# A fused attention, dense and routed feed-forward kernel: where its routing constants stand, how it inverts the softmax sums, and when it asks for raw weights

## The chip, the cores and the metric

The kernel runs on one core of one Trainium2 chip, as one launch. The metric is the device time of the launch in microseconds (us). The engines are written as the profile writes them: PE (matrix multiply), DVE (vector), ACT (scalar), POOL (general purpose), SP (here it only issues DMAs). The engines run side by side; each works through its own instructions in a fixed order, and an instruction that waits holds up all that stand behind it on the same engine.

## What is computed

Three stages in a row. Attention comes first, for 4 batches of 8 heads, 576 positions, head size 64:

```python
scores = scale * np.matmul(q, k.transpose(0, 1, 3, 2))
bias = -(cum[:, :, :, None] - cum[:, :, None, :])
scores = np.where(causal, -1000000000.0, scores + np.minimum(bias, 0.0))
attn = np.exp(scores - np.max(scores, axis=-1, keepdims=True))
attn = attn / (np.sum(attn, axis=-1, keepdims=True) + 1e-09)
return np.matmul(attn, v)
```

Its output, 2,304 tokens of 512 numbers, goes through a dense layer, `max(x @ w1, x @ w2, x @ w3) @ w_out`, and then through a routed one: each token goes to the one of 8 experts with the largest `x @ w_gate + modality_bias[modality_id]`. The weights of the dense layer arrive as raw 64-bit words and are taken apart on the chip.

## The kernel before

The work on attention goes by couples of heads: 16 couples (`p` from 0 to 15), two heads each. For a head, `load` (L190) asks SP for q and k (`qk_r`, 576 KB) and one augmented row for `k_b`; `split` (L206) makes high and low parts on ACT, POOL and DVE (L210 to L214); `scores` (L222) multiplies on PE into one PSUM bank after another (L242, L243; three banks take turns), DVE adds the mask and finds the least value of each row (L244, its result `mn`), and ACT takes the exponential and sums each row (L246). The sums of a couple stand in one tile `l`: 128 rows, two heads, five query chunks. `turned` (L270) transposes a head's exponentials on PE (L275, 15 blocks), and DVE and ACT copy them out of PSUM in turn (L278, L280). `values_of` (L286) multiplies them with v (L298), and DVE scales the product with the inverse sums `rb` (L299, L300).

`inverse` (L253) makes `rb`. POOL writes ones into a part of a tile `r` (L255), DVE adds 1e-9 to the sums in two instructions (L256, L257) and takes the reciprocal of 128 rows of 10 numbers (L258), PE transposes (L260), ACT copies the ten rows of 128 out (L262), and SP writes them to DRAM (L263) and reads them back spread over 64 rows for each head (L266). `queue` calls it as soon as a couple's second head has its scores; `drain` (L353) does the transposes and values one couple behind.

`convert` (L115) takes one block of the dense weights apart: SP loads the raw words (L117, 512 KB, two buffers), ACT scales (L122), DVE shifts and merges (L123 to L125), POOL casts by a DMA (L127) and subtracts (L130). The table `CONV` (L83) says behind which couple which of the first nine blocks is done; load and conversion stand together there. A block of code that begins at L369 sets up the constants of the routing: seven DMAs on SP, four instructions on POOL, seven on DVE, among them three on the biases (L394 to L396), which need `mb_sb` (L392). It stands in the program right behind the first couple.

Once four couples are done, parts of the dense layer (`fill`, L315, with L143 to L147 and L323) are put between the heads as filler for PE; their places are tied to score matmuls. The rest of the dense layer, the routing and the experts follow the last couple.

The order on each engine isn't the program's order: a scheduler lays the instructions out engine by engine when the kernel is built, after what depends on what and its own estimate of times. `tc.issue_after(x)` asks it to keep what a block issues behind instruction `x`.

Of the kernel before, what the change touches and what calls it, by code (L numbers as in the profile page):

```python
# [5 lines left out]
F32 = mybir.dt.float32  # L6
F32R = mybir.dt.float32r
BF16 = mybir.dt.bfloat16
I32 = mybir.dt.int32
# [70 lines left out]
E_N = 4  # L80
RAW_BUFS = 2
R2_BUFS = 4
CONV = {2: [0, 1], 3: [2], 4: [3, 4], 5: [5], 7: [6], 8: [7], 9: [8]}  # L83


def fused_kernel(tc, qk, vd, sd, w64, mod, wg, wgt, mb, we, cst, csi, out):
# [3 lines left out]
    with top:  # L90
# [24 lines left out]
        def convert(f, k, pool, tag, rp_, early=False):  # L115
            raw = rp_.tile([128, 512, 2], I32, tag="raw", name="w_raw")
            SP.dma_start(out=raw.rearrange("p n c -> p (n c)"), in_=w64[f, :, k * 512:(k + 1) * 512].bitcast(I32))  # L117
            h = pool.tile([128, 512], F32R, tag=tag, name="w_h")
            lo = pool.tile([128, 512], F32R, tag=tag, name="w_l")
            z = zsp.tile([128, 512], F32, name="w_z")  # L120
            zi = z.bitcast(I32)
            A.activation(out=z, in_=raw.bitcast(F32)[:, :, 1], func=ACTF.Abs, scale=2.0 ** -112)  # L122
            V.tensor_scalar(out=zi, in0=zi, scalar1=3, scalar2=None, op0=ALU.logical_shift_left)  # L123
            V.scalar_tensor_tensor(out=zi, in0=raw[:, :, 0], scalar=29, in1=zi, op0=ALU.logical_shift_right, op1=ALU.bitwise_or)
            V.scalar_tensor_tensor(out=zi, in0=raw[:, :, 1], scalar=-2 ** 31, in1=zi, op0=ALU.bitwise_and, op1=ALU.bitwise_or)  # L125
            if early and W_DMA:
# [24 lines left out]
        with ExitStack() as es:  # L151
# [99 lines left out]


            def inverse(p, l):  # L253
                r = ss.tile([128, 2, 5], F32, name="r")
                G.memset(r[0:64, :, 0:1], 1.0)  # L255
                V.tensor_scalar(out=r[64:128, :, 0:1], in0=l[0:64, :, 0:1], scalar1=1e-9, scalar2=None, op0=ALU.add)  # L256
                V.tensor_scalar(out=r[:, :, 1:5], in0=l[:, :, 1:5], scalar1=1e-9, scalar2=None, op0=ALU.add)  # L257
                V.reciprocal(out=r, in_=r)  # L258
                r_ps = ps_t.tile([128, 512], F32, name="t_ps")[0:10, 0:128]
                P.transpose(out=r_ps, in_=r.rearrange("p j c -> p (j c)"), identity=ident)  # L260
                r_t = ss.tile([10, 128], F32, name="r_t")
                A.copy(out=r_t, in_=r_ps)  # L262
# [23 lines left out]
            def values_of(p, v_r, rb, pts):  # L286
# [13 lines left out]
                V.tensor_tensor(out=xb[b][:, hp, 0:64], in0=o_0[:, 0:64], in1=rb[:, 64:128], op=ALU.mult)  # L300


            def fill_x(i, pool, tag, on=None):
# [48 lines left out]

            def drain(keep):  # L353
                while len(behind) > keep:
                    p, es_, v_r, rb, pts = behind.pop(0)
                    pts.append(turned(es_[len(pts)], len(pts)))
                    if len(pts) == 2:
                        values_of(p, v_r, rb, pts)


            def queue(p, es_, v_r):
                rb = inverse(p, sums[-1])
                pts = []
                behind.extend((p, es_, v_r, rb, pts) for _ in range(2))

            queue(0, [front(j) for j in range(2)], vv)


            tri_f = ap1.tile([128, 128], F32, name="tri_f")  # L369
            SP.dma_start(out=tri_f, in_=cst[:, 128:256])  # L370
            G.tensor_copy(out=tri, in_=tri_f)
            G.memset(ones, 1.0)
            G.memset(acc[:, 0, :], 0.0)
            SP.dma_start(out=off, in_=cst[:, 384:384 + E])
            SP.dma_start(out=iota, in_=cst[:, 392:456])
            sent = ap1.tile([128, TABLE // 128, 2], F32, name="sent")
            G.memset(sent, 0.0)
            G.memset(sent.bitcast(I32)[:, :, 0:1], SENT)
            SP.dma_start(out=table.rearrange("(p n) c -> p n c", p=128), in_=sent)
            tok = ap1.tile([128, NT], I32, name="tok")  # L380
            SP.dma_start(out=tok, in_=csi)
            V.tensor_copy(out=meta.bitcast(I32)[:, :, 0], in_=tok)
            mod_i = ap1.tile([128, NT, 2], I32, name="mod_i")
            SP.dma_start(out=mod_i, in_=mod)
            mod_b = ap1.tile([128, NT], I32, name="mod_b")
            V.tensor_scalar(out=mod_b, in0=mod_i[:, :, 0], scalar1=1, scalar2=None, op0=ALU.bitwise_and)
            m1 = ap1.tile([128, NT], F32, name="m1")
            V.tensor_copy(out=m1, in_=mod_b)
            m0 = ap1.tile([128, NT], F32, name="m0")
            V.tensor_scalar(out=m0, in0=m1, scalar1=-1.0, scalar2=1.0, op0=ALU.mult, op1=ALU.add)  # L390
            mb_sb = ap1.tile([128, 2, E], F32, name="mb_sb")
            SP.dma_start(out=mb_sb, in_=mb.to_broadcast([128, 2, E]))  # L392
            bias0 = ap1.tile([128, NT, E], F32, name="bias0")
            V.tensor_tensor(out=bias, in0=m1.unsqueeze(2).to_broadcast([128, NT, E]), in1=mb_sb[:, 1:2, :].to_broadcast([128, NT, E]), op=ALU.mult)  # L394
            V.tensor_tensor(out=bias0, in0=m0.unsqueeze(2).to_broadcast([128, NT, E]), in1=mb_sb[:, 0:1, :].to_broadcast([128, NT, E]), op=ALU.mult)
            V.tensor_tensor(out=bias, in0=bias, in1=bias0, op=ALU.add)  # L396

            todo = []
            n_head = 2
            for p in range(1, NP):  # L400
                v_r = values_in(p)
                es_ = []
                for j in range(2):
                    es_.append(front(2 * p + j))
                    drain(1 - j)
                    if j == 1:
                        queue(p, es_, v_r)
                    n_head += 1
# [4 lines left out]
                if p == NP - 1:  # L413
                    drain(0)
# [480 lines left out]
```

## Time and profile before

| what | us |
|---|---|
| runs | 760.15, 761.93, 2,456.17 |
| median of the runs | 761.93 |
| the profiled execution, its own time | 757.26 |
| its span, first to last instruction | 755.4 |
| PE busy in the span | 718.7 |
| DVE busy | 533.2 |
| ACT busy | 404.6 |
| POOL busy | 179.4 |

The span is what the profile shows of the device time; 1.9 us lie around it. A busy PE is one with a matmul in flight; whether its clock was at its upper level (2.4 GHz, written 1.00) or its lower (1.2 GHz, 0.50) stands beside it as the granted clock.

### The profile page before, as it was taken

To read this page: it belongs to the slowest core of one execution; us is meant where nothing else is said; L and a number is where in the kernel's file an instruction comes from. 1 tells how busy PE (TensorE), PEld (TensorE's weight loads), DVE (VectorE), ACT (ScalarE), POOL (GpSimd) and SP (SyncE) were. 2 spreads that over 40 slices of the span, in tenths; PEclk is the share of its full clock that TensorE was granted. 3 is DMA by queue.
4 is the path that set the end of the run, shared out by engine and by line. 5 is a ranking of instruction groups with operands and counts; after the bars stand their busy time and mean duration, and the time that the engine had idled before them with its cause. 6 is when DMAs were issued, how large, how long until landed. Compare 5 with 4: busy or idle time off the path is not lost. (4 is left out here: it accounts for less than half of the span.)

```text
span 755.4 us, 13659 instructions
## 1 busy us (share of the span) xinstructions
PE 718.7 (95%) x4602; PEld 640.3 (85%) x4602; DVE 533.2 (71%) x1599; ACT 404.6 (54%) x976; POOL 179.4 (24%) x218
## 2 busy tenths in 40 slices
PE   4887999998999999999999999999999999999996
PEld 3665789887889899999898998998899888999884
DVE  6888998987866579594676886756777556576540
ACT  6885778776757535312222222445647555575531
POOL 6344554543322100001010101032132122121101
PEclk9998999999999999999999999999999999999999
DMA  7566646675412164110101011566648575756610
GB/s 221 158 229 182 194 150 191 175 243 154 125 65 79 35 236 170 45 37 12 53 11 64 22 49 22 204 221 177 236 121 274 196 255 181 259 211 203 210 62 18
DMA packets 45105, 108.56 MB, mean 144 GB/s; under 512 B 8993, under 2 KB 12993, under 8 KB 45025
## 3 DMA queue, kind: packets, MB, share of 16 engines
q1 hardware_dynamic: 37368, 90.75, 37.8%
q0 software_dynamic: 4912, 11.82, 4.9%
q10 hardware_dynamic: 2744, 5.02, 1.8%
q8 instruction: 38, 0.62, 0.3%
q14 instruction: 43, 0.34, 0.2%
HBM read 93.55 MB, written 12.18 MB: 140 GB/s over the span
## 5 line engine op out<-in xcount | busy, mean ns | idle before, releaser
L143 PE MATMUL a_ps<-xh,w_h 128*128 128x384 f32 (+2 forms) x492 | 159.8, 325 | 4.4 <-DVE h L323 3.4
L146 PE MATMUL a_ps<-xl,w_h 128*128 128x384 f32 (+2 forms) x492 | 158.2, 322 | 0.2 <-POOL xl L312 0.2
L147 PE MATMUL a_ps<-xh,w_l 128*128 128x384 f32 (+2 forms) x492 | 157.0, 320 | 0.0
L595 DVE TENSOR_TENSOR e_l<-e_raw,e_h 128x512 fp32r<-128x512 f32 x160 | 102.9, 688 | 15.7 <-ACT e_h L594 13.8
L246 ACT ACTIVATE e<-e,mn 128x64 f32<-128x64 f32 (+4 forms) x160 | 88.9, 557 | 32.4 <-DVE mn L244 32.1
L594 ACT CAST e_h<-e_raw 128x512 fp32r<-128x512 f32 x160 | 92.8, 622 | 20.3 <-DMA e_raw<-in_we 10.2
L143 PEld LDWEIGHTS a_ps<-xh,w_h 128*128 128x128 f32 x492 | 92.7, 188 | 7.0 <-DVE h L323 4.1
L146 PEld LDWEIGHTS a_ps<-xl,w_h 128*128 128x128 f32 x492 | 92.8, 189 | 0.8 <-POOL xl L312 0.4
L147 PEld LDWEIGHTS a_ps<-xh,w_l 128*128 128x128 f32 x492 | 92.6, 188 | 0.1
L242 PE MATMUL s_ps<-hl 128*128 128x64 f32 (+2 forms) x192 | 67.0, 361 | 15.2 <-DVE hl L213 9.0
L628 PE MATMUL h_ps<-x2t,e_h 128*128 128x256 f32 x288 | 81.2, 283 | 0.0
L629 PE MATMUL h_ps<-x2t,e_l 128*128 128x256 f32 x288 | 80.9, 282 | 0.0
L625 PE MATMUL h_ps<-x2t,e_h 128*128 128x256 f32 x288 | 80.0, 282 | 0.2 <-issue 0.2
L482 DVE CUSTOM_DVE_ANT_0 junk<-x,wg 128x512 bf16<-128x512 f32 x96 | 65.9, 687 | 17.2 <-ACT x L556 16.2
L275 PE MATMUL t_ps<-ident,e 128*128 128x128 f32 x480 | 69.6, 279 | 7.2 <-DVE pt L278 3.1
L506 POOL DMA_INDIRECT table<-meta,si x18 | 19.9, 1108 | 230.6 <-DVE mx L486 90.5
L244 DVE CUSTOM_DVE_ANT_0 e<-s_ps,mask 128x64 f32<-128x64 f32 (+4 forms) x160 | 63.2, 424 | 5.6 <-PE s_ps L243 4.4
L275 PEld LDWEIGHTS t_ps<-ident,e 128*128 128x128 f32 x480 | 56.6, 143 | 11.0 <-DVE pt L278 4.4
L656 PE MATMUL y_ps<-e_h,gh 128*128 128x512 f32 x152 | 61.3, 403 | 0.4 <-ACT gh L648 0.4
L243 PE MATMUL s_ps<-k_b,q_b 66*128 66x64 f32 (+2 forms) x192 | 60.2, 326 | 0.6 <-DMA k_b<-augk 0.6
L658 PE MATMUL y_ps<-e_h,gl 128*128 128x512 f32 x152 | 60.7, 399 | 0.0
L657 PE MATMUL y_ps<-e_l,gh 128*128 128x512 f32 x152 | 59.9, 394 | 0.0
(179 smaller groups left out, 1478.4 us busy)
## 6 DMA issues: line engine op xcount, KB each, us to landing
e_raw<-in_we SPq DMA_DIRECT2D x80, 512.0 KB
qk_r<-in_qk SPq DMA_DIRECT2D x30, 576.0 KB
w_raw<-in_w SPq DMA_DIRECT2D x24, 512.0 KB
v_r<-in_vd SPq DMA_DIRECT2D x16, 320.0 KB
rb<-r_d SPq DMA_DIRECT2D x32, 160.0 KB
x2d<-x ACTq DMA_DIRECT2D x18, 256.0 KB
w_h<-w_z POOLq DMA_DIRECT2D x9, 256.0 KB, 4.5
wg<-in_wg SPq DMA_DIRECT2D x4, 512.0 KB
```

The source lines that it names most:

```text
L143: ins = P.matmul(a_ps, wh[:, c], xh[:, c], start=c == 0, stop=False).ins
L146: P.matmul(a_ps, wh[:, c], xl[:, c], start=False, stop=False)
L147: P.matmul(a_ps, wl[:, c], xh[:, c], start=False, stop=c == 3)
L242: P.matmul(s_ps, hl[:, 1, q0:q0 + nq], hl[:, 0, k0:k0 + n], start=True, stop=False)
L246: ex = A.activation(out=ec, in_=ec, func=ACTF.Exp, bias=mn[0:nq, c:c + 1], scale=-1.0, accum_out=l[0:nq, c:c + 1]).ins
L275: last_t[0] = P.transpose(out=t_ps[:, n * 128:(n + 1) * 128], in_=e[:, EOFF[c] + kb * 128:EOFF[c] + (kb + 1) * 128], identity=ident).ins
L482: V.tensor_tensor_reduce(out=junk, in0=x2, in1=wg_sb[ei // 2][:, ei % 2, :], scale=1.0, scalar=0.0, op0=ALU.mult, op1=ALU.add, accum_out=l ...
L594: A.copy(out=h, in_=raw[:, a])
L595: V.tensor_tensor(out=lo, in0=raw[:, a], in1=h.bitcast(F32), op=ALU.subtract)
L625: ins = P.matmul(h_ps, w(hs, f, c), xt[:, 0, c], start=c == 0, stop=False).ins
L628: P.matmul(h_ps, w(hs, f, c), xt[:, 1, c], start=False, stop=False)
L629: P.matmul(h_ps, w(ls, f, c), xt[:, 0, c], start=False, stop=c == 3)
```

## The change

Three edits in the attention stage.

1. The routing constants become a function `tables()`, which is called behind couple 12 in a block that is to be issued after the last exponential so far (`exps[-1]`, an instruction of ACT).
2. `inverse` transposes the sums themselves. ACT adds the 1e-9 as it copies the transposed sums out of PSUM, and DVE takes the reciprocal there, of 10 rows of 128 numbers. POOL's fill with ones and DVE's two additions are gone. It is called one head later: behind the next couple's first head (for the last couple, at the end). The scaling of the first chunk reads `rb[:, 0:64]` in place of `rb[:, 64:128]`.
3. `convert` is cut in two. The load of the raw words stands one couple ahead of the conversion (`CONV` moves by one, the conversions stay where they were).

```diff
-CONV = {2: [0, 1], 3: [2], 4: [3, 4], 5: [5], 7: [6], 8: [7], 9: [8]}
+CONV = {1: [0, 1], 2: [2], 3: [3, 4], 4: [5], 6: [6], 7: [7], 8: [8]}
+P_SET = 12
...
             SP.dma_start(out=raw.rearrange("p n c -> p (n c)"), in_=w64[f, :, k * 512:(k + 1) * 512].bitcast(I32))
+            if not early:
+                converted(f, k, pool, tag, raw)
+            return f, k, pool, tag, raw, True
+
+        def converted(f, k, pool, tag, raw, early=False):
...
             def inverse(p, l):
-                r = ss.tile([128, 2, 5], F32, name="r")
-                G.memset(r[0:64, :, 0:1], 1.0)
-                V.tensor_scalar(out=r[64:128, :, 0:1], in0=l[0:64, :, 0:1], scalar1=1e-9, scalar2=None, op0=ALU.add)
-                V.tensor_scalar(out=r[:, :, 1:5], in0=l[:, :, 1:5], scalar1=1e-9, scalar2=None, op0=ALU.add)
-                V.reciprocal(out=r, in_=r)
...
-                P.transpose(out=r_ps, in_=r.rearrange("p j c -> p (j c)"), identity=ident)
+                P.transpose(out=r_ps, in_=l.rearrange("p j c -> p (j c)"), identity=ident)
                 r_t = ss.tile([10, 128], F32, name="r_t")
-                A.copy(out=r_t, in_=r_ps)
+                A.activation(out=r_t, in_=r_ps, func=ACTF.Copy, bias=1e-9)
+                V.reciprocal(out=r_t, in_=r_t)
...
+                return lambda: rbs.append(inverse(p, l))
...
                     es_.append(front(2 * p + j))
+                    if j == 0:
+                        turn()
                     drain(1 - j)
                     if j == 1:
-                        queue(p, es_, v_r)
+                        turn = queue(p, es_, v_r)
...
-                for n in CONV.get(p, ()):
-                    with tc.issue_after(exps[-1 - CONV_LAG]), tc.issue_after(last_load[0]):
-                        convert(n // 3, n % 3, w0p, "w0", rawp, early=True)
+                with tc.issue_after(exps[-1 - CONV_LAG]), tc.issue_after(last_load[0]):
+                    for w in raws:
+                        converted(*w)
+                    raws = [convert(n // 3, n % 3, w0p, "w0", rawp, early=True) for n in CONV.get(p, ())]
+                if p == P_SET:
+                    with tc.issue_after(exps[-1]):
+                        tables()
```

What the scheduler made of it stands below, at three places; line numbers are those of the kernel the rows belong to.

On DVE, in the scores of the second head of all (`e_133`; `e_134` is the third), where the biases of the routing are made. Before:

```order
L394 TENSOR_TENSOR bias<-m_297,mb_sb 128x144
L395 TENSOR_TENSOR bias_303<-m_299,mb_sb 128x144
L256 TENSOR_SCALAR r<-l 64x2
L244 ISA e_133,mn<-s_ps,mask 128x288
L244 ISA mn 128x1
L396 TENSOR_TENSOR bias<-bias,bias_303 128x144
```

In the changed kernel:

```order
L395 TENSOR_SCALAR m_2812<-m_2810 128x18
L399 TENSOR_TENSOR bias<-m_2810,mb_sb 128x144
L250 ISA e_133,mn<-s_ps,mask,mn 128x288
L250 ISA mn 128x1
L400 TENSOR_TENSOR bias_2816<-m_2812,mb_sb 128x144
L250 ISA e_134,mn<-s_ps,mask 128x64
```

The biases (now L399 and L400) are still made in the second head of all, some instructions further down and no longer both in a row.

On SP, from the read-back of an inverse (`rb`) to the first raw weights (`w_raw`). Before, from the loads ahead of the second couple's inverse on:

```order
L201 DMA qk_r<-in_qk 128x2x576 x2
L219 DMA v_r<-in_vd 128x640
L263 DMA r_d<-r_t 10x128
L202 DMA k_b<-dk 2x576
L266 DMA rb<-r_d 64x640 x2
L117 DMA w_raw<-in_w 128x1024 x2
```

In the changed kernel, from the first couple's read-back on:

```order
L268 DMA rb<-r_d 64x640 x2
L118 DMA w_raw<-in_w 128x1024 x2
L207 DMA qk_r<-in_qk 128x2x576 x2
L225 DMA v_r<-in_vd 128x640
L208 DMA k_b<-dk 2x576
L265 DMA r_d<-r_t 10x128
```

The first two raw blocks are asked for a couple earlier, ahead of two heads' q and k that stood before them.

On PE, where the first inverse and the first transposes stand. Before, in the fourth head's scores:

```order
L242 MATMUL s_ps<-hl 128x192
L243 MATMUL s_ps<-k_b,q_b_129 128x192
L242 MATMUL s_ps<-hl 128x320
L243 MATMUL s_ps<-k_b,q_b_129 128x320
L260 MATMUL t_ps<-ident,r 10x128
L275 MATMUL t_ps<-ident,e_132 128x128 x8
```

In the changed kernel, between the third head's scores and the fourth's:

```order
L248 MATMUL s_ps<-hl 128x288
L249 MATMUL s_ps<-k_b,q_b_131 128x288
L261 MATMUL t_ps<-ident,l 10x128
L277 MATMUL t_ps<-ident,e_132 128x128 x8
L248 MATMUL s_ps<-hl 128x64
L249 MATMUL s_ps<-k_b,q_b_129 128x64
```

The transposes begin half a head earlier; those of the sums come from `l`, no longer from `r`.

## Rows read from the trace of the kernel before

**Rows 1.** Stretches: start:end length, busy PE, PEld, DVE, ACT, POOL, clock, DMA share, GB/s.

```profile
0.00:20.00 20.00, 8.71 (x26) 6.54 (x26) 12.95 (x34) 14.26 (x32) 13.65 (x43) 1.00 0.75 221
20.00:40.00 20.00, 17.47 (x102) 14.30 (x103) 17.71 (x65) 17.48 (x50) 7.85 (x9) 1.00 0.50 160
40.00:60.00 20.00, 15.50 (x117) 12.27 (x117) 16.92 (x51) 16.11 (x44) 9.04 (x10) 0.99 0.72 221
60.00:80.00 20.00, 16.66 (x104) 11.48 (x101) 16.45 (x49) 13.04 (x37) 9.47 (x11) 0.84 0.58 176
...
100.00:120.00 20.00, 19.99 (x158) 18.11 (x157) 17.91 (x59) 17.63 (x52) 11.98 (x13) 1.00 0.48 150
```

**Rows 2.** Waits of PE over the span: us in total, times, longest.

```profile
PE s_ps L242 <- DVE hl L213: 9.0, 1, 9.0
PE s_ps L242 <- DVE mn L244: 6.0, 8, 1.8
```

**Rows 3.** Timeline of PE, the longest gaps elsewhere: start, us, instruction, idle before it.

```profile
46.53 0.40 PE L242 MATMUL s_ps<-hl 128*128 128x288 f32 x1 [1.69 <-DVE mn L244]
...
71.88 1.09 PE L275 MATMUL t_ps<-ident,e 128*128 128x128 f32 x8 [3.08 <-DVE pt L278]
...
173.31 0.40 PE L143 MATMUL a_ps<-xh,w_h 128*128 128x288 f32 x1 [2.33 <-DVE h L323]
```

**Rows 4.** Timeline from 11 to 22 us: third split, first bias, PE's gap.

```profile
11.99 1.38 DVE L213 TENSOR_TENSOR hl<-qk_r,hl 64x576 fp32r<-64x576 f32 x1 [0.37 <-ACT hl L210]
...
19.84 0.31 DVE L394 TENSOR_TENSOR bias<-m,mb_sb 128x144 f32<-128x144 f32 x1 [1.25 <-DMA mb_sb<-in_mb]
...
21.12 0.53 PE L242 MATMUL s_ps<-hl 128*128 128x192 f32 x1 [1.77 <-DVE mn L244]
```

**Rows 5.** Timeline from 45 to 54 us: the first raw weights and who waits.

```profile
45.17 1.05 SPq L117 DMA_DIRECT2D w_raw<-in_w  x2
...
52.15 0.43 DVE L123 TENSOR_SCALAR w_z<-w_z 128x512 int32<-128x512 int32 x1 [2.81 <-ACT w_z L122]
...
53.36 0.66 PE L275 MATMUL t_ps<-ident,e 128*128 128x128 f32 x4 [1.56 <-DVE x L300]
```

**Rows 6.** The same table by 2 us, two of the stretches from 58 to 82 us.

```profile
60.00:62.00 2.00, 2.00 (x6) 0.47 (x4) 1.87 (x8) 0.81 (x3) 1.14 (x1) 0.50 0.96 273
...
74.00:76.00 2.00, 2.00 (x11) 1.97 (x11) 1.94 (x8) 1.22 (x5) 0.26 (x1) 0.50 0.94 336
```

**Rows 7.** Tile r, the inverse: duration ns min/median/max, first and last start; idle ahead.

```profile
L256 DVE TENSOR_SCALAR r<-l x16: 161/163/1239, 20.4 to 242.7; 64x2 f32<-64x2 f32 x16
L257 DVE TENSOR_SCALAR r<-l x16: 160/172/1081, 24.6 to 248.8; 128x8 f32<-128x8 f32 x16
L258 DVE RECIPROCAL r<-r x16: 204/216/217, 25.3 to 249.0; 128x10 f32<-128x10 f32 x16
...
  ACT e L246: 4.5, 8
```

**Rows 8.** Timeline from 28 to 43 us: the way of the first inverse, and a load.

```profile
28.21 0.27 SPq L263 DMA_DIRECT2D r_d<-r_t  x1
...
29.91 1.14 SPq L266 DMA_DIRECT2D rb<-r_d  x2
31.15 0.58 SPq L201 DMA_DIRECT2D qk_r<-in_qk  x1
...
38.71 0.69 DVE L299 TENSOR_TENSOR x<-o_ps,rb 128x512 f32<-128x512 f32 x1
...
42.20 0.67 ACT L210 CAST hl<-qk_r 64x576 fp32r<-64x576 f32 x1
```

**Rows 9.** Timeline from 66 to 71 us: DVE and POOL before PE's longest gap.

```profile
66.82 2.60 DVE L124 SCALAR_TENSOR_TENSOR w_z<-w_raw,w_z 128x512 int32<-128x512 int32 x1
68.84 1.83 POOL L214 TENSOR_TENSOR q_b<-qk_r,hl 64x576 fp32r<-64x576 f32 x1
69.45 1.84 DVE L213 TENSOR_TENSOR hl<-qk_r,hl 64x576 fp32r<-64x576 f32 x1
```

More of the change, by code (lines that the diff above doesn't have):

```diff
@@ L299, in values_of @@
                 V.tensor_tensor(out=xb[b][:, hp, 64:S], in0=o_ps, in1=rb[:, 128:640], op=ALU.mult)
-                V.tensor_tensor(out=xb[b][:, hp, 0:64], in0=o_0[:, 0:64], in1=rb[:, 64:128], op=ALU.mult)
+                V.tensor_tensor(out=xb[b][:, hp, 0:64], in0=o_0[:, 0:64], in1=rb[:, 0:64], op=ALU.mult)
             def fill_x(i, pool, tag, on=None):
@@ L354, in drain @@
                 while len(behind) > keep:
-                    p, es_, v_r, rb, pts = behind.pop(0)
+                    p, es_, v_r, rbs, pts = behind.pop(0)
                     pts.append(turned(es_[len(pts)], len(pts)))
                     if len(pts) == 2:
-                        values_of(p, v_r, rb, pts)
+                        values_of(p, v_r, rbs[0], pts)
             def queue(p, es_, v_r):
-                rb = inverse(p, sums[-1])
                 pts = []
-                behind.extend((p, es_, v_r, rb, pts) for _ in range(2))
@@ L366, in fused_kernel @@
[L366 to L394, printed above, removed]
@@ L395, in fused_kernel, with tables @@
-            V.tensor_tensor(out=bias0, in0=m0.unsqueeze(2).to_broadcast([128, NT, E]), in1=mb_sb[:, 0:1, :].to_broadcast([128, NT, E]), op=ALU.mult)
-            V.tensor_tensor(out=bias, in0=bias, in1=bias0, op=ALU.add)
+                rbs = []
+                l = sums[-1]
+                behind.extend((p, es_, v_r, rbs, pts) for _ in range(2))
+                return lambda: rbs.append(inverse(p, l))
+            turn = queue(0, [front(j) for j in range(2)], vv)
+            def tables():
+                tri_f = ap1.tile([128, 128], F32, name="tri_f")
+                SP.dma_start(out=tri_f, in_=cst[:, 128:256])
+                G.tensor_copy(out=tri, in_=tri_f)
+                G.memset(ones, 1.0)
+                G.memset(acc[:, 0, :], 0.0)
+                SP.dma_start(out=off, in_=cst[:, 384:384 + E])
+                SP.dma_start(out=iota, in_=cst[:, 392:456])
+                sent = ap1.tile([128, TABLE // 128, 2], F32, name="sent")
+                G.memset(sent, 0.0)
+                G.memset(sent.bitcast(I32)[:, :, 0:1], SENT)
+                SP.dma_start(out=table.rearrange("(p n) c -> p n c", p=128), in_=sent)
+                tok = ap1.tile([128, NT], I32, name="tok")
+                SP.dma_start(out=tok, in_=csi)
+                V.tensor_copy(out=meta.bitcast(I32)[:, :, 0], in_=tok)
+                mod_i = ap1.tile([128, NT, 2], I32, name="mod_i")
+                SP.dma_start(out=mod_i, in_=mod)
+                mod_b = ap1.tile([128, NT], I32, name="mod_b")
+                V.tensor_scalar(out=mod_b, in0=mod_i[:, :, 0], scalar1=1, scalar2=None, op0=ALU.bitwise_and)
+                m1 = ap1.tile([128, NT], F32, name="m1")
+                V.tensor_copy(out=m1, in_=mod_b)
+                m0 = ap1.tile([128, NT], F32, name="m0")
+                V.tensor_scalar(out=m0, in0=m1, scalar1=-1.0, scalar2=1.0, op0=ALU.mult, op1=ALU.add)
+                mb_sb = ap1.tile([128, 2, E], F32, name="mb_sb")
+                SP.dma_start(out=mb_sb, in_=mb.to_broadcast([128, 2, E]))
+                bias0 = ap1.tile([128, NT, E], F32, name="bias0")
+                V.tensor_tensor(out=bias, in0=m1.unsqueeze(2).to_broadcast([128, NT, E]), in1=mb_sb[:, 1:2, :].to_broadcast([128, NT, E]), op=ALU.mult)
+                V.tensor_tensor(out=bias0, in0=m0.unsqueeze(2).to_broadcast([128, NT, E]), in1=mb_sb[:, 0:1, :].to_broadcast([128, NT, E]), op=ALU.mult)
+                V.tensor_tensor(out=bias, in0=bias, in1=bias0, op=ALU.add)
@@ L398, in fused_kernel @@
+            raws = []
             todo = []
@@ L413, in fused_kernel @@
                 if p == NP - 1:
+                    turn()
                     drain(0)
-                for n in CONV.get(p, ()):
-                    with tc.issue_after(exps[-1 - CONV_LAG]), tc.issue_after(last_load[0]):
-                        convert(n // 3, n % 3, w0p, "w0", rawp, early=True)
+                with tc.issue_after(exps[-1 - CONV_LAG]), tc.issue_after(last_load[0]):
[5 more added lines that the diff above has]
+                        tables()
                 if p % (H // 2) == H // 2 - 1:
```

## The prediction

> **What bounds the kernel now.** I read the busy times first: PE works 718.7 of the 755.4 us of the span (they stand in the table of times), and the change takes no matmul away, so only PE's idle time (36.7 us) and the time it spends at its lower clock can be won. The table by stretches tells where that idle time lies: PE is busy 8.71, 17.47, 15.50 and 16.66 us in the first four stretches of 20 us, and 19.99 from 100 to 120 us, where pieces of the dense layer fill its gaps [rows 1]. So the change must earn its time in the first 80 us or so. Next come the waits of PE: 9.0 us are the start, before anything can be multiplied, and 6.0 us in 8 waits are for DVE's `mn`, which frees the score banks [rows 2]. The timeline of PE shows the rest one by one: 1.77 us at 21, 1.69 at 46.5, 1.56 at 53, 3.08 at 72, 2.33 at 173 [rows 3 to 5]. DVE stands behind each; it is itself busy 16 to 18 of every 20 us there [rows 1]. Last I read the clock: from 60 to 80 us the granted clock is 0.84 on average [rows 1]. With levels of 1.00 and 0.50 that is 6.4 us at the lower one, which cost 3.2 us; finer stretches show them in two pieces, about 60 and about 75 us, at 0.50 [rows 6]. I take 1.6 us for each; both follow stretches in which PE had waited.
>
> **The change part by part.** The sum is made against the profiled execution, 757.26 us (755.4 of span and 1.9 around it); the median of the runs lies 4.7 us above it.
>
> *Constants of the routing.* The order on DVE shows that they don't move: `tables()` waits on an instruction of ACT and issues nothing on ACT, and its biases still stand in the second head. What does move is small. Before, DVE sat 1.25 us on `mb_sb`, which SP asks for behind two other loads; then PE stood 1.77 us [rows 4]. In the new order SP asks for it one load earlier and DVE comes to it later: I count −1.3 (from 0 to −1.8). Against that the third head's `hl` (L213, 1.38 us [rows 4]) now stands ahead of the first score pass instead of behind it: +0.7 (0 to 1.4). And the second couple's v, 320 KB, is asked for where a small table stood; at the 221 GB/s of that stretch [rows 1] it is 1.5 us of transfer, which mostly hides behind the chain that starts PE: +0.5 (0 to 1.5). Together 0 (−1.8 to +2.9). All else in `tables()`, its DMAs and POOL's fills, stays in its place.
>
> *Inverse.* Each couple loses three DVE instructions of 0.163, 0.172 and 0.216 us in the median [rows 7], 0.55 in all, and gains one reciprocal over 128 numbers a row where 10 were. No row shows that one. From below: the bias product goes over 144 numbers in 0.31 us [rows 4], so 0.28 if a reciprocal were as quick per number. From above: 0.216 × 12.8 = 2.8 us if all of the short one's time grew with its length. I take 0.85: the additions take 0.16 us at their least, so 0.16 is fixed and the 0.054 us that the reciprocal takes beyond it for 10 numbers make 0.69 for 128. That is +0.30 a couple (−0.27 to +2.2). It counts only where DVE holds PE up, in the first five couples: +1.5 (−1.4 to +11). On the other side DVE no longer waits for the last exponential before the additions: 4.5 us of idle time in 16 couples [rows 7], 1.4 in five (0 to −1.4). The sums' way gets one step longer (PE, ACT, DVE, SP, DRAM, SP) and starts a head later; from the write at 28.21 and the read-back at 29.91 to the use of `rb` at 38.71 lie 10.5 us [rows 8], of which the new order, with a head's scores and the values between, leaves enough. Cost nothing; if that cover is gone, DVE stands at L299 with the next scores behind it, and PE waits for a bank. POOL's fills of 0.1 us hold nobody. PE gets the first transposes half a head earlier, work to do while DVE lags: −0.8 (0 to −1.7, the gap at 46.5 us [rows 3]). Together −0.7.
>
> The Trainium skill speaks against this edit ("VectorE: DVE Perf Modes", section "First, the fixed hardware budget"): the reciprocal is an iterative division with a repeat count of 8. By that, and the 0.96 GHz of its specifications, 128 numbers take an estimated 1.07 us besides the fixed part, so 1.2 us; the sum below would be 1.8 us worse. The row bears it out by half: ten numbers cost 0.054 us beyond the fixed part, and by the rule it would be 0.083.
>
> *Raw weights a couple earlier.* SP asked for the first two blocks at 45.17 us; ACT and then DVE stood for them, DVE 2.81 us, and behind DVE PE 1.56 us [rows 5]. In the new order they are asked for behind the first couple's read-back, so at some 31 us [rows 8], long before ACT wants them. That wait goes: −1.6. The first piece of lower clock follows it; I give that an even chance to go with it: −0.8 (0 to −1.6). The two blocks now stand ahead of two heads' q and k. Before, such a load was asked for at 31.15 and used by ACT at 42.20 [rows 8], 11 us; another 1 MB at 160 to 221 GB/s [rows 1] takes 4.7 to 6.6 of these, and the load's own 576 KB up to 3.7. That still fits: 0 (up to +3). Together −2.4 (−3.2 to +1.4).
>
> *What stands elsewhere for it.* The 3.08 us at 72 come from one collision: a merge of raw words (L124) took 2.60 us and the `hl` behind it 1.84, while POOL ran beside them [rows 9]. Those instructions now meet other partners; half of the wait and half of the second piece of lower clock: −1.5 and −0.8 (together 0 to −4.7). The same for the wait of 2.33 us at 173, in another conversion: −1.0 (0 to −2.3). But a new order makes new collisions; five such waits sum to 10.4 us now, 2.1 each, and I add one: +2.1 (0 to +6).
>
> **Sum:** 0 − 0.7 − 2.4 − 3.3 + 2.1 = −4.3 us. From 757.26 that is 753.0; from the median, 757.6, which is my forecast. From about 100 us on PE is full and its order hardly differs, so nothing is added there.
>
> **The rivals.**
>
> *The waits are dealt anew.* Every gap goes and comes back elsewhere, because DVE is as busy as before (up by 0.30 a couple) and only its order differs. For it: its 16 to 18 of 20 us [rows 1]. Against it: the stalls on two transfers [rows 4, 5] have a cause of their own that is gone. It gives the old time, 762 (760 to 765).
>
> *The long reciprocal makes DVE later still.* Slower than before. At 1.8 us, the middle of 0.85 and 2.8, each couple costs DVE 1.25 us more, 6.2 in five couples; the gain of the raw weights' wait takes back 1.6, so +4.6: 766.5. It decides from the point where five couples' extra outweighs 2.4 us, at 0.48 us a couple, a reciprocal of 1.03 us, if no collision goes. For it: DVE is the engine that PE waits for, and the new place puts the reciprocal between score passes. Against it: the short one's excess of 0.054 us [rows 7] is small.
>
> *All early waits go.* The five waits of 10.4 us and both pieces of lower clock, 3.2: −13.6, 748.3. For it: one wait makes the next, since PE falls to the lower clock behind it. Against it: two of the five are collisions which the change doesn't aim at.
>
> That the change doesn't do what its name says is no rival any more for the routing constants; the order shows it. If the order had moved them, the gain would be the 1.8 us of PE's gap there, and the start's transfers would be fewer.
>
> **How the numbers follow.** The forecast, 753.5 to 760.5 by itself, gets 0.50, the waits dealt anew 0.22, the long reciprocal 0.15, all early waits 0.13. Leaving out a part of the two outer cases, the time should lie between 749.5 and 767 us. Within 2% means 746.7 to 777.2 us, about what a measurement of this kernel can tell from no change. PE's idle time in the first 80 us without the start (21.7 − 9.0 [rows 1, 2]), the wait at 173 us and the lower clock come to 18.2 us, 2.4%, so faster by more than 2% gets 0.05; slower by more would need the upper bound of the reciprocal on most couples, 0.03; within 2%, 0.92.
>
> **What would show each step right or wrong.** The constants: the biases still near 20 us, with no wait on `mb_sb` ahead of them. The inverse: the mean of the new reciprocal, 0.85 us by my count and over 1.03 for the slower rival; no DVE wait for `rb` ahead of L301. The raw weights: no wait of ACT on `w_raw` at the first two blocks; a wait of the split on `qk_r` near 40 us would show that they push the heads' loads back. The collisions: PE's waits of over 1.5 us behind the start, 10.4 us now, should sum to some 6, and the granted clock from 60 to 80 us should rise above 0.84. The forecast is wrong if PE's busy time changes by more than the clock explains, or if the time moves after 100 us.

## The result

The changed kernel takes 751.05 us in the median of four runs (749.54 to 752.56), beside 761.04 for the kernel before on the same chip (759.73 to 761.93 without one run of 2456.17). The ratio, worked out from the means without that run and not from these medians, is 0.9874, with an interval from 0.9841 to 0.9908. That is faster, by less than the 2% that the forecast called faster. It lies inside the forecast's range (749.5 to 767) and 6.5 us under its number (757.6). The profiled execution took 752.2 us, 750.3 of it span, against 757.26 and 755.4.

The table by stretches answers to [rows 1]; its columns are the same.

```profile
0.00:20.00 20.00, 7.79 (x24) 6.21 (x24) 13.00 (x32) 13.41 (x29) 13.15 (x39) 1.00 0.82 243
20.00:40.00 20.00, 17.42 (x99) 14.50 (x100) 15.86 (x56) 15.49 (x44) 6.56 (x7) 1.00 0.48 147
40.00:60.00 20.00, 16.94 (x118) 12.46 (x116) 19.43 (x57) 16.92 (x49) 8.97 (x10) 1.00 0.62 199
60.00:80.00 20.00, 18.37 (x122) 12.39 (x123) 19.29 (x46) 15.50 (x42) 13.72 (x13) 0.91 0.69 213
...
100.00:120.00 20.00, 19.69 (x151) 17.20 (x152) 16.32 (x52) 16.73 (x47) 9.35 (x10) 1.00 0.57 175
```

The start is no better: PE works 25.2 us in the first 40, before 26.2. The difference lies from 40 to 80 us, where PE is busy for 35.3 us instead of 32.2, at a better clock. The column to look at is DVE's, the third of the busy times: 19.4 and 19.3 of 20 us, where it was 16.9 and 16.5. Over the whole span DVE is busy for 529.4 us, before for 533.2, so it has hardly less to do; from 40 to 80 us it gets more of it done, because it itself waits less.

The waits of PE over the span, as in [rows 2] (us in total, times, longest):

```profile
PE s_ps L248 <- DVE hl L219: 9.2, 1, 9.2
PE s_ps L248 <- DVE mn L250: 6.4, 9, 1.7
PE o_ps L300 <- ACT pt L282: 2.5, 2, 1.5
PE t_ps L277 <- DVE pt L280: 1.6, 3, 0.7
```

And the gaps of PE of over 1 us from 20 us on, from its timeline, as in [rows 3] and the last of [rows 4, 5] (start, us, instruction, idle before it):

```profile
25.01 0.61 PE L248 MATMUL s_ps<-hl 128*128 128x288 f32 x1 [1.26 <-DVE mn L250]
...
35.25 2.81 PE L300 MATMUL o_ps<-pt,v_r 128*64 128x512 f32 x20 [1.04 <-ACT pt L282]
...
60.88 4.51 PE L300 MATMUL o_ps<-pt,v_r 128*64 128x512 f32 x20 [1.51 <-ACT pt L282]
...
149.22 0.42 PE L248 MATMUL s_ps<-hl 128*128 128x320 f32 x1 [1.18 <-DVE mn L250]
```

The waits for `mn` are as long as before in sum. What is gone are the five gaps that the prediction named, at 21, 46.5, 53, 72 and 173 us; of over 1.5 us only one remains there. Of the two gaps behind a conversion, for `x` and for `h`, neither comes in this execution. But that differs between executions: a second profile of the same kernel (after_again, below) has one for `x` again, later than before's at 53 us:

```profile
67.52 0.66 PE L277 MATMUL t_ps<-ident,e 128*128 128x128 f32 x4 [2.58 <-DVE x L302]
```

The parts show in the tiles. For the constants (engine, form, duration ns min/median/max, first and last start):

```profile
L397 SPq DMA_DIRECT2D mb_sb<-in_mb x1: 432/432/432, 14.7 to 14.7; - x1
L399 DVE TENSOR_TENSOR bias<-m,mb_sb x1: 296/296/296, 20.8 to 20.8; 128x144 f32<-128x144 f32 x1
```

They stand where they stood, near 20 us, and no wait on `mb_sb` is left. For the inverse, the group of its reciprocal (count | busy us, mean ns | idle ahead), and of tile `rb` its first reader and DVE's idle time ahead of all its readers:

```profile
L264 DVE RECIPROCAL r_t<-r_t 10x128 f32<-10x128 f32 x16 | 14.9, 934 | 0.2 <-ACT r_t L263 0.2
```

```profile
L301 DVE TENSOR_TENSOR x<-o_ps,rb x16: 677/692/693, 38.1 to 261.4; 128x512 f32<-128x512 f32 x16
...
  PE o_ps L300: 18.1, 10
```

The reciprocal takes 0.93 us. `rb` itself is never waited for, but DVE now stands for PE's values, 18.1 us in 10 waits (7.8 in 5 before). For the raw weights, the load, and ACT's waits on it:

```profile
L118 SPq DMA_DIRECT2D w_raw<-in_w x24: 327/362/589, 33.9 to 288.8; - x24
L128 ACT ACTIVATE w_z<-w_raw x24: 653/671/697, 42.7 to 298.2; 128x512 f32<-128x512 f32 x24
...
  DMA w_raw<-in_w: 2.6, 2
```

The first is asked for at 33.9 us and used at 42.7; ACT waits for such loads 2.6 us in 2, where it was 8.0 in 7.

Last the clock, as in [rows 6], with stretches of the same table from further back:

```profile
60.00:62.00 2.00, 1.12 (x4) 0.45 (x6) 1.61 (x1) 1.95 (x4) 1.98 (x3) 0.75 0.92 254
74.00:76.00 2.00, 1.77 (x10) 0.93 (x12) 2.00 (x9) 1.95 (x5) 1.29 (x2) 1.00 0.23 78
500.00:510.00 10.00, 9.32 (x52) 8.13 (x51) 5.65 (x33) 4.90 (x12) 3.29 (x4) 0.83 0.24 78
...
540.00:550.00 10.00, 9.79 (x65) 9.53 (x64) 5.71 (x31) 4.40 (x11) 5.02 (x5) 0.71 0.32 106
```

One early piece of lower clock is left, at 61 to 65 us, and the one at 75 is gone. But there are pieces between 500 and 550 us, where the profile of before shows 1.00. The change does nothing there: at 511 us, by the last matmul into `b_ps`, the kernel was 7.6 us ahead, at the end 5.1.

**One account for all kernels.** Taken together, the profiles give a simple sum. A stretch whose granted clock is 0.83 lacks 17% of its length. Summed over a span these missing parts are 4.8 us before and 8.4 after. PE's busy time less this loss is 713.9 us before and 711.2 after, and in 13 of the 14 profiles of this study it lies between 709 and 714 (707.5 in set_moved, below). So a span is some 711 us of PE's work, plus PE's idle time, plus the loss at the lower clock. Each run lists its span and its mean granted clock, so both can be had from all runs and not the profiled ones alone: the loss is the span times what the clock lacks of 1, and the span without it is 711 us and the idle time. (Where PE idles at the lower clock the loss is counted too high: in all 14 profiles the clock also falls at the very end, behind the last matmul, which counts 0.6 to 2.2 us and costs nothing.) For 81 runs of before in this study the means are 749.8 and 8.3; for ten of the changed kernel 741.8 and 6.3. Five more runs of before, of 764.9 to 767.6 us, count as slow, over 1.5% above its fastest, and are left out, while no run of another kernel is; with the five in, the ratios on two of the chips would be lower by up to 0.001. **The change takes some 8.0 us off the span without loss, and 2.0 us of lower clock.** A difference in the span without loss is called idle time below, but it is that only within some 3 us: of the 8.6 us by which the two profiles differ in it, 6.0 are idle time of PE (36.7 before, 30.7 after) and the rest is PE's own work, which is not quite the same in every profile. Why it isn't stays open. The loss differs much from run to run, 1.5 to 13.7 us before; the times of these runs lie between 753.4 and 764.4 us. The means of a kernel in the table below carry an error of 0.2 to 1.0 us.

### The profile page after: what moved, and what is told of

Its sections match the earlier page's. It is cut to its first block, busy times and chain, and to the rows that moved or that the text cites. A ratio compares the mean times of both kernels' runs of the same rounds, so it can differ in the third digit from the quotient of the medians.

```text
span 750.3 us, 13624 instructions
## 1 busy us (share of the span) xinstructions
PE 719.6 (96%) x4602; PEld 642.7 (86%) x4602; DVE 529.4 (71%) x1567; ACT 404.4 (54%) x976; POOL 181.6 (24%) x202
## 5 line engine op out<-in xcount | busy, mean ns | idle before, releaser
L495 DVE CUSTOM_DVE_ANT_0 junk<-x,wg 128x512 bf16<-128x512 f32 x96 | 66.0, 688 | 16.9 <-ACT x L569 16.0
L277 PE MATMUL t_ps<-ident,e 128*128 128x128 f32 x480 | 71.4, 280 | 2.2 <-DVE pt L280 1.6
```

What stands on the lines that cost most here:

```text
L277: last_t[0] = P.transpose(out=t_ps[:, n * 128:(n + 1) * 128], in_=e[:, EOFF[c] + kb * 128:EOFF[c] + (kb + 1) * 128], identity=ident).ins
L495: V.tensor_tensor_reduce(out=junk, in0=x2, in1=wg_sb[ei // 2][:, ei % 2, :], scale=1.0, scalar=0.0, op0=ALU.mult, op1=ALU.add, accum_out=l ...
```

## The experiments

The theory to be tested was the prediction's: each part takes away its own waits, and the prices add. Against it stood that a scheduler orders every engine's stream anew at each edit, so that the gain belongs to the one order that came out. The table has all results; "form" and "delay" are the two halves of the inverse's part, its new form and its later place (time: median, us; ratio to the kernel before on the same chip, with its 95% interval, again not the quotient of the medians; then the two means, span without loss, and loss, us).

| kernel | raw | inverse | constants | time | ratio | span − loss | loss |
|---|---|---|---|---|---|---|---|
| before | | | | 759.4 to 760.6 | 1 | 749.8 | 8.3 |
| raw_only | x | | | 761.19 | 1.0041 (1.0009 to 1.0072) | 747.8 | 12.3 |
| inv_only | | x | | 762.71 | 1.0056 (1.0027 to 1.0085) | 749.1 | 12.0 |
| tab_only | | | x | 756.11 | 0.9969 (0.9942 to 0.9996) | 745.8 | 8.7 |
| raw_tab | x | | x | 763.21 | 1.0030 (1.0002 to 1.0059) | 749.4 | 11.4 |
| inv_tab | | x | x | 761.52 | 1.0030 (1.0003 to 1.0057) | 749.2 | 11.5 |
| no_tab | x | x | | 749.09 | 0.9865 (0.9827 to 0.9902) | 741.2 | 6.1 |
| after_again | x | x | x | 748.98 | 0.9875 (0.9840 to 0.9910) | 741.8 | 5.5 |
| turn_first | x | x | x | 751.25 | 0.9894 (0.9855 to 0.9932) | 742.6 | 6.7 |
| set_moved | x | x | truly | 760.01 | 1.0002 (0.9977 to 1.0026) | 743.9 | 14.5 |
| raw_form | x | form | | 763.38 | 1.0049 (1.0017 to 1.0081) | 746.9 | 15.1 |
| raw_delay | x | delay | | 763.72 | 1.0060 (1.0028 to 1.0091) | 749.1 | 13.1 |
| short_recip | x | other | x | 762.25 | 1.0032 (1.0003 to 1.0062) | 749.5 | 10.9 |

### The parts one by one

**raw_only**: the kernel before with the raw weights' part of the change.

```diff
-CONV = {2: [0, 1], 3: [2], 4: [3, 4], 5: [5], 7: [6], 8: [7], 9: [8]}
+CONV = {1: [0, 1], 2: [2], 3: [3, 4], 4: [5], 6: [6], 7: [7], 8: [8]}
...
+                    for w in raws:
+                        converted(*w)
+                    raws = [convert(n // 3, n % 3, w0p, "w0", rawp, early=True) for n in CONV.get(p, ())]
```

> Only the raw weights of the dense layer are asked for a couple ahead; the inverse and the routing constants are as in the kernel before. Theory 1 (each gain belongs to the wait that the prediction named): ACT's waits on w_raw fall from 8.0 us in 7 to about 2.6 in 2, PE's wait of 1.56 us at 53 us and a piece of lower clock go, 756 to 759 us, ratio 0.994 to 0.997. Theory 2 (most of the gain is a new dealing of the order, which any edit brings): the waits on w_raw go all the same, but the time may lie anywhere between 755 and 765 us, and other waits take their place. Theory 3 (the raw weights are the whole of the gain): 751 us, ratio 0.987.

It is slower, by 0.4%. Its own waits go (PE's 1.56 us at 53 is not there, the idle time, as counted above, falls by 2.0 us), but other waits come, and with them the clock falls more often. The table by stretches from 40 to 100 us, and the waits of DVE from 40 to 160:

```profile
40.00:100.00 60.00, 49.90 (x316) 37.94 (x315) 53.62 (x149) 43.77 (x120) 29.18 (x33) 0.89 0.60 182
```

```profile
DVE e L250 <- PE s_ps L249: 4.3, 6, 1.7
DVE x L305 <- PE o_ps L304: 2.9, 2, 2.7
```

A clock of 0.89 over 60 us is a loss of 6.6; in the profile of before the same stretch has 0.94. DVE now waits for PE, at its lower clock, and PE for DVE: 6.7 us in 6 waits for `mn` alone from 40 to 240 us, before 2.6 in 4.

**inv_only**: the inverse's part, form and delay.

```diff
-                r = ss.tile([128, 2, 5], F32, name="r")
...
+                P.transpose(out=r_ps, in_=l.rearrange("p j c -> p (j c)"), identity=ident)
...
+                V.reciprocal(out=r_t, in_=r_t)
...
+                    if j == 0:
+                        turn()
```

> Only the inverse of the sums is in its new form and a head later; the raw weights and the routing constants are as in the kernel before. Theory 1 (by the prediction's terms, with the reciprocal at the 0.93 us that the trace of the changed kernel shows): DVE does 0.38 us more a couple and waits 4.5 us less for the last exponential: 759 to 762 us, ratio 0.997 to 1.002. Theory 2 (the order dealt anew): 755 to 765 us with waits of PE in other places. Theory 3 (DVE's waits for the sums and for rb were the main thing): 754 us or less, ratio 0.991 or less.

Slower by 0.6%, where theory 1 allowed 0.2 at most. The idle time, as counted above, is 0.7 us less, which is the prediction's own number for this part; the loss is 3.7 us more. Two rows of DVE's waits from 40 to 160 us show where it stands:

```profile
DVE w_z L124 <- ACT w_z L123: 7.2, 4, 4.2
DVE e L245 <- PE s_ps L244: 3.5, 3, 1.9
```

The raw weights are late as before (there 5.7 us in 4), and DVE also stands for score passes of PE, whose clock is at 0.91 in this stretch from 40 to 100 us.

**tab_only**: the code of the routing constants behind couple 12, in a function.

```diff
+                if p == P_SET:
+                    with tc.issue_after(exps[-1]):
+                        tables()
```

> Only the code of the routing constants is where the change put it; inverse and raw weights are as in the kernel before. Theory 1: the biases stay near 20 us, the wait on mb_sb goes, and the time stays: 759.5 to 763 us, ratio 0.998 to 1.002. Theory 2 (the order dealt anew): the same constants, but the order of the score and transpose passes differs from there on, and the time moves by up to 4 us in either direction. Theory 3 (the start gives the gain: the couples from 30 us on run earlier): 757 us or less, ratio 0.995 or less.

0.3% faster, with 4.0 us less idle time and the same loss: theory 2 or 3. The constants stay near 20 us here too. The first thing that the edit moves is one load: v of the second couple goes ahead of `tri_f` on SP. From there on the streams differ on every engine; on PE, by the traces, 347 of 4,602 matmuls stand elsewhere than before. That this one load sets off the rest is not shown.

**after_again**: the changed kernel once more.

> The changed kernel as it is, once more, beside its parts on one chip: ratio 0.984 to 0.991. For the pieces of lower clock between 500 and 550 us: if they belong to the kernel's order they come again in this profile with the same 5 us; if they come by chance in one execution, the stretches from 500 to 550 us show a granted clock of 1.00 and this execution is about 4 us shorter than the profiled 752.2.

Its ratio comes again. Late in the span the first profile lost 1.7 us at 504 us and 3.4 at 538; this one loses 1.7 us at 539 alone, and no_tab, below, nothing there. The stretch from 540 to 550 us in after_again:

```profile
540.00:550.00 10.00, 9.83 (x76) 9.64 (x75) 7.05 (x33) 4.76 (x12) 5.47 (x5) 0.87 0.34 107
```

and in no_tab:

```profile
540.00:550.00 10.00, 9.76 (x79) 9.35 (x78) 7.74 (x38) 4.28 (x12) 4.92 (x5) 1.00 0.42 102
```

So they come by chance, in one execution and not in the next.

### The parts in pairs

**no_tab**: the change without its first part.

```diff
+            tables()
             raws = []
...
-                if p == P_SET:
-                    with tc.issue_after(exps[-1]):
-                        tables()
```

> The raw weights a couple ahead and the new inverse together, the routing constants in their old place: the changed kernel without its first part. Theory 1 (each part has its own price, and prices add): the two alone measured 1.004 and 1.006, so together 1.010, 767 us. Theory 2 (the parts act through the order that the scheduler deals; this kernel's order differs from the changed kernel's in few rows): 0.985 to 0.993, 748 to 754 us, with PE idle and lower clock as in the changed kernel. Theory 3 (the routing constants' part carries the gain, by the earlier v): 757 us or more, ratio 0.997 or more.

The whole gain, from two parts that each make the kernel slower. Theory 1 said 767 us; it falls here. The two rows that tell it, stretches of 40 to 100 and 100 to 240 us:

```profile
40.00:100.00 60.00, 51.18 (x365) 40.52 (x366) 57.45 (x154) 46.29 (x129) 30.75 (x30) 0.97 0.64 194
100.00:240.00 140.00, 137.81 (x1082) 121.78 (x1081) 110.66 (x340) 104.91 (x300) 57.56 (x57) 1.00 0.47 150
```

DVE works 57.5 of 60 us, as in the changed kernel (57.2), and the clock lacks 3%, one piece. Yet this execution has two long waits of PE there, of 2.59 us at 66 and 2.13 at 74, and 8.8 us of idle time in this stretch, as before (9.0): what sets its profile apart from that of before is 2.4 us less of lower clock, 1.9 us less idle time from 100 to 240 us (2.2 for 4.1), and 2.6 us less of PE's own work, which nothing here explains.

**raw_tab** and **inv_tab**: the change with the old inverse, and with the old places of the raw weights' loads.

```diff
-                A.activation(out=r_t, in_=r_ps, func=ACTF.Copy, bias=1e-9)
-                V.reciprocal(out=r_t, in_=r_t)
...
+                V.reciprocal(out=r, in_=r)
```

> The raw weights and the routing constants as in the change, the inverse as in the kernel before. Theory 1 (prices add): 1.0041 times 0.9969, so 1.001, 760 us. Theory 2 (the order decides): an order of its own, anywhere from 0.985 to 1.010; whatever it gives is explained by PE's idle time and the lower clock between 40 and 240 us, and the PE work at full clock that remains is the same 711 us as in the other kernels, within 2. Theory 3 (the new inverse with raw weights is what counts): not under 0.995.

```diff
-                    for w in raws:
-                        converted(*w)
...
+                        convert(n // 3, n % 3, w0p, "w0", rawp, early=True)
```

> The inverse and the routing constants as in the change, the raw weights asked for as before. Theory 1 (prices add): 1.0056 times 0.9969, so 1.0025, 761 us. Theory 2 (the order decides): anywhere from 0.985 to 1.010, and again 711 us of PE work at full clock within 2, the rest being idle time and lower clock. Theory 3 (the raw weights are needed for the gain): not under 0.995, with waits of ACT and DVE on w_raw near 45 to 55 us that PE pays.

Both are 0.3% slower than before. Sums of prices would have given 1.001 and 1.0025, which the intervals don't exclude; but the 4.0 us of idle time that tab_only gained are not there, in either. Of PE's work at full clock the profiles show 710.3 and 713.1, as expected. So the gain needs the raw weights and the inverse together, or it needs an order that these two together happen to give.

### The same parts in another order

**set_moved**: the constants truly behind couple 12.

```diff
-                    with tc.issue_after(exps[-1]):
+                    with tc.issue_after(last_load[0]), tc.issue_after(last_v[0]), tc.issue_after(last_g[0]):
                         tables()
```

> The changed kernel with the routing constants truly behind couple 12: they wait for instructions of SP, DVE and POOL there, and not for one of ACT alone. The start then has no biases on DVE and fewer loads. Theory 1 (the start's work counts): biases come behind 120 us, PE is busier from 0 to 40 us by 1 to 2 us than the 25.2 of the changed kernel, and the time falls to 747 to 750 us, 0.983 to 0.987. Theory 2 (the order decides): PE's start gains the same, but from 40 us on the order is another, and the total may be 0.980 to 1.005.

The start was to be better. PE is busy 26.5 us of the first 40, 1.3 more, but a piece of lower clock at 32 us takes 3.4, more than that, and the time comes out as before: 1.0002. The stretch from 40 to 100 us, and one row of DVE's waits from 40 to 160:

```profile
40.00:100.00 60.00, 50.32 (x315) 38.68 (x313) 54.21 (x142) 42.07 (x118) 25.50 (x27) 0.86 0.59 171
```

```profile
DVE x L304 <- PE o_ps L303: 12.9, 6, 3.5
```

In the changed kernel this wait is 3.6 us in 3. The scaling by `rb` stands in DVE's stream where PE has not got to the values yet, and the score passes queue behind it. That it is these score passes that then make PE wait is argued, not shown. The loss before 240 us is 13.7 us. This kernel has both parts that the gain seemed to need, and lighter work at the start, and no gain in time. By the means it is not all lost: its span without loss is 5.9 us under that of before, three quarters of the changed kernel's 8.0, and the lower clock takes 6.2 us back.

**turn_first**: one call moved by one head's code; every engine keeps its instructions.

```diff
                 for j in range(2):
+                    if j == 0:
+                        turn()
                     es_.append(front(2 * p + j))
-                    if j == 0:
-                        turn()
```

> The changed kernel with one call moved: the inverse of a couple is asked for just ahead of the next couple's first head instead of just behind it. Every engine gets the same instructions; the order of PE differs in 224 of some 5,300 rows. Theory 1 (the raw weights and the new inverse carry the gain by what they take off the engines): 0.984 to 0.992, as with the changed kernel. Theory 2 (the gain is a property of the one order that came out): 0.985 to 1.005, and what it differs from the changed kernel by is PE's idle time from 40 to 240 us and 1.7 us for each piece of lower clock.

0.9894: the gain stays. This one counts for theory 1, or for an order that is near enough; by its interval it can't be told from the changed kernel.

**raw_form** and **raw_delay**: no_tab with half of the inverse undone. The first asks for the new form at once, the second has the old form a head later.

```diff
-                        turn = queue(p, es_, v_r)
+                        queue(p, es_, v_r)()
```

> Raw weights a couple ahead and the new form of the inverse, but asked for at once behind its couple and not a head later; routing constants as before. If the head's delay is what keeps DVE and PE from waiting on the last exponential and the read-back, the gain goes: 0.997 to 1.005. If the form (three DVE instructions fewer) and the raw weights suffice: 0.985 to 0.992. By the order alone: 0.985 to 1.010, explained by idle time and pieces of lower clock.

```diff
-                V.reciprocal(out=r_t, in_=r_t)
...
+                V.reciprocal(out=r, in_=r)
```

> Raw weights a couple ahead and the inverse in its old form (additions, short reciprocal, transpose) but a head later; routing constants as before. If the delay and the raw weights suffice: 0.985 to 0.992. If the form is needed: 0.997 to 1.005. By the order alone: 0.985 to 1.010, explained by idle time and pieces of lower clock.

Neither half suffices; both are among the slowest kernels of the study. In raw_form it is nearly all one wait (PE, 40 to 240 us), and the clock from 100 to 240 lacks 5%, more than in any other:

```profile
PE s_ps L248 <- DVE mn L250: 13.1, 10, 2.8
PE t_ps L277 <- DVE pt L280: 1.0, 1, 1.0
```

```profile
100.00:240.00 140.00, 134.22 (x1001) 116.54 (x1000) 107.18 (x315) 98.88 (x277) 60.29 (x57) 0.95 0.49 149
```

**short_recip**: the changed kernel with the reciprocal ahead of the transpose. It leaves out the addition of 1e-9.

```diff
+                r = ss.tile([128, 2, 5], F32, name="r")
+                V.reciprocal(out=r, in_=l)
...
-                A.activation(out=r_t, in_=r_ps, func=ACTF.Copy, bias=1e-9)
-                V.reciprocal(out=r_t, in_=r_t)
+                A.copy(out=r_t, in_=r_ps)
```

> The changed kernel with the reciprocal taken ahead of the transpose, over ten numbers a row (0.216 us by the kernel before) instead of over 128 (0.93 us), without the addition of 1e-9, which is lost in sums of at least 1. DVE has 0.72 us less a couple, 11 us in all and 3.6 us in the first five couples. If DVE's time is what PE pays there: 745 to 748 us, 0.979 to 0.984, faster than both kernels. By the order that is dealt anew: 0.985 to 1.005, with the DVE time saved all the same.

DVE's time is saved, as the group of the reciprocal shows, 3.4 us in all instead of 14.9:

```profile
L261 DVE RECIPROCAL r<-l 128x10 f32<-128x10 f32 x16 | 3.4, 212 | 0.7 <-ACT e L252 0.6
```

But DVE's busy time as a whole hardly falls: 528.5 us, beside 529.4 in the changed kernel. Other instructions of DVE take longer here; the low parts `hl` show it, first in the changed kernel, then here:

```profile
L219 DVE TENSOR_TENSOR hl<-qk_r,hl 64x576 fp32r<-64x576 f32 x32 | 30.3, 946 | 4.0 <-ACT hl L216 3.0
...
L219 DVE TENSOR_TENSOR hl<-qk_r,hl 64x576 fp32r<-64x576 f32 x32 | 34.6, 1083 | 4.5 <-ACT hl L216 3.6
```

So the run doesn't tell what less work on DVE in all would bring. The kernel is not faster than before (1.0003 to 1.0062), and PE waits 8.1 us for `mn` from 40 to 240 us (2.9 in the changed kernel). The best idea on paper is worth nothing in the order that it got. So no version beat the changed kernel: no_tab equals it.

**What follows.** Shown is: the prices of the parts don't add; the difference between these kernels is, within some 3 us, idle time of PE, most of it in the heads' phase, and lower clock that follows such idle time; and a shorter reciprocal (short_recip) or less work at the start (set_moved) doesn't bring the gain. The three kernels that have it, after_again, no_tab and turn_first, are also those whose orders are close: by the traces, of 4,602 matmuls 13 stand elsewhere in no_tab than in the changed kernel and 149 in turn_first, in the other kernels 281 to 393 (317 in the kernel before). That is what theory 2 wants. Open is which rows of the order do it, and whether a kernel with the two parts in yet another order, with nothing else touched, would lose the gain: turn_first was meant to ask that and came out too near. That the order is the cause is thus argued by exclusion, not shown by a swap of the order alone.

## Why the prediction was right or wrong

**The time.** The range held it, the narrower forecast of 753.5 to 760.5, to which the prediction gave 0.50, did not. Against the profiled executions, on which the sum was made, −4.3 us stands beside −5.1: close, but by luck. The execution profiled of before had a loss of 4.8 us where 8.3 is the mean, and that of the changed kernel 8.4 where 6.3 is. By the means it was −8.0 of idle time and −2.0 of loss; the prediction's terms, sorted in the same way, are −2.7 and −1.6. The gain in idle time is what was too small.

**Constants.** That they don't move was right (biases at 20.8 us), and so was 0 for them: no_tab and after_again are the same. What moves around them was read rightly too: no wait on `mb_sb`, v earlier, a later first pass; the first 40 us are 1.0 us worse, inside the bounds of −1.8 to +2.9. That the part alone gains 0.3% was not foreseen.

**Inverse.** The reciprocal was taken at 0.85 us (bounds 0.28 to 2.8) and measured 0.934. The Trainium skill ("VectorE: DVE Perf Modes", section "First, the fixed hardware budget") has a repeat count of 8 for it, by which, at the 0.96 GHz of its specifications, an estimate is 1.2 us in all. The measurement lies between. From 10 numbers in 0.216 us to 128 in 0.934 it is 6.1 ns a number, under the 8.3 that this rule makes at 0.96 GHz. The point from which the rival with the long reciprocal decides, 1.03 us, was not reached. What the additions had cost was read too low: the prediction took their medians, 0.55 us a couple with the reciprocal, but a few are far longer (up to 1.24 us, as its own row shows), and all three sum to 12.4 us beside the new reciprocal's 14.9. So DVE has 0.16 us more a couple, not 0.30 or, with the measured reciprocal, 0.38. By itself the part cuts the idle time by 0.7 us, as its term had it, within an error of 0.7; what the prediction lacked is that it brings 3.7 us of lower clock when alone. That `rb` would not be waited for was right; that DVE would stand for `o_ps` instead, 18.1 us, was not seen.

**Raw weights.** The step was right in its mechanism: the wait of ACT, of DVE and the 1.56 us of PE are gone, the loads ahead of q and k cost 0.5 us (PE's wait for `qk_r` at 48 us). Its −1.6 of idle time alone measured −2.0. But the even chance that a piece of lower clock goes with it was wrong in its sign for the part alone: the loss rose by 4.0 us.

**Elsewhere.** Half of the wait at 72 us, half of the second piece of lower clock and 1.0 of the 2.3 us at 173 were counted; all three went whole in the profiled execution. +2.1 was counted for new collisions, one wait of the old size. The five old waits, 10.4 us, went, but PE's idle time fell by only 6.0 us (3.8 in after_again), so 4.4 to 6.6 us of new waiting came: more than the term, though mostly in shorter pieces. The old waits had been counted at 6.2 of their 10.4 us, so both terms were too small, and the two misses partly cancelled. From 40 to 100 us the idle time fell from 9.0 to 5.1 us (7.5 in after_again).

**"Nothing is added from about 100 us on"** is the step that failed. From 100 to 240 us PE's idle time fell from 4.1 to 2.2 us and to 500 by another 0.8, in the two profiles; both of the changed kernel have the same. Of these 2.7 us the prediction had counted 1.0, for the wait at 173 us, against its own sentence. The order there does differ: the two streams on PE differ again and again from the first heads to the last.

**The rivals.** As far as the runs show, "The waits are dealt anew" described the mechanism best, and was wrong in that it gave the old time: a new deal isn't neutral, it gave anything from −1.3% to +0.6%. "All early waits go" came nearer with its number (748.3) than the forecast. The sum over parts, the method of the prediction, can't have been right for this kernel: with the parts' measured prices it would have given 1.0041 × 1.0056 × 0.9969, so 1.007.

## What to carry to other kernels

Where a scheduler writes each engine's stream, an edit has two effects: the wait that it aims at, and a new deal of all others; here the sums of the parts' prices missed the measured times by up to 2.3%, and the deal is the explanation that is left, though not shown by itself. So price an edit by its own waits, but give the deal a range of its own, measure parts together as well as alone, and don't drop a part because it is slower by itself. And compare means over runs of PE's idle time and of the loss at the lower clock, not two profiled executions alone: the loss by itself is anything from 1.5 to 13.7 us in runs of the kernel before.

## What the runs showed of the hardware that was not expected

The lower clock comes in pieces of one price. In all 14 profiles a piece ahead of the last matmul lacks 1.7 us of its length, or twice or four times that, and every one follows idle time of PE; in the changed kernel the pieces at 504 and 538 us follow gaps of 0.7 us only. The same two gaps are in the profiles of before and of no_tab without a fall. Before 240 us the profiles of the changed kernel, no_tab, turn_first and tab_only have one such price to pay, that of before two, and the others four to eight. The reciprocal's price per number, 6.1 ns, is the other thing: ten numbers on 128 rows take 0.216 us, so that turning the sums first, to work on ten rows, makes the one instruction four times as long.
